# Stage one of a two-stage sequence kernel: one chunk of 128 tokens, or pairs of chunks with two tokens in a partition

## The chip, the cores and the metric

The kernel runs on one core of one Trainium2 chip. The time is that of the device in microseconds (us), from the runs of one program; a profile is one execution taken by the hardware profiler. The engines are PE (TensorE, matrix products), DVE (VectorE), ACT (ScalarE), POOL (GpSimd) and SP (SyncE, which issues most transfers). [...]

## The reference

Two layers stand one behind the other, on 4 batches, 768 tokens, 8 heads of 48 channels. The first is a recurrence with a decayed state; the second a gated long convolution, done with a Fourier transform over the tokens.

```python
for t in range(S):
    cur = np.einsum('bhd,bhe->bhde', u[None] * kt, vt)
    y[:, :, t] = np.einsum('bhd,bhde->bhe', rt, state + cur)
    state = wt[:, :, :, None] * state + np.einsum('bhd,bhe->bhde', kt, vt)
...
proj = x @ w_proj                       # (b, s, 3 * 384) -> x1, x2, x3
x2_conv = irfft(rfft(x2) * rfft(filter))
out = (x1 * x2_conv * x3) @ w_out
```

## The kernel before

**Stage one** takes the tokens in 24 chunks of 128, six a batch, with a token in each partition. For one chunk the program's steps have these names, which also stand in the order below:

- `lw`, `lk`, `lr`, `lv` load w, k, r and v (192 KB each). In the memory a token's 48 channels of one head lie together, so a load is made of packets of 192 bytes (`group`, L1425 to L1438). From the third group on, half of the v loads are issued by GpSimd and turned to bf16 on the way.
- `ln` takes the logarithm of w (ACT); `cs` sums it over the tokens of the chunk with two products by a triangular mask, 128 x 384 each, and four products of one column that give the whole chunk's decay (PE, L1473 to L1476); `ex` takes the exponential in PSUM (ACT); `kq` multiplies it by k and r (DVE, L1486); `ph` makes the decay of the state.
- `tr` turns keys and queries with eight transposes (PE, L1501), and `qk` copies them out of PSUM (ACT or DVE). For the last eight chunks a DMA on SP's queue may do both.
- `sc` makes the scores, eight products of 48 rows, two heads side by side in the two halves of the array's rows (PE, L1519). `mt` copies them with the mask (DVE) or without, and then `mc` cuts them on GpSimd.
- `kv` and `ki` make the next state (PE, L1560, L1566), `su` decays it (DVE).
- `rk`, `ru`, `rh`, `cc`, `vc` work out the token's own term with u (GpSimd and DVE).
- `yi`, `ys`, `y` add up the output in PSUM: the token's own term, the state's part and the scores times the values (PE, L1580, L1589, L1597). `xn` copies it out, `yt` turns it, `xT` stores it as the input of stage two, for some of the last chunks again by DMA.

**Stage two** works a batch at a time, once its six chunks are there: `p` and `q` project x1 and x3 (PE, L1768), `xw` projects x2 with tokens in partitions (L1809), `sd` folds the two halves of the sequence, `f` is the Fourier transform (L1655), `u` and `p<batch>` the product with the filter's spectrum, `E` the inverse transform (L1865), `aE`, `dE`, `yE` put its halves together and gate them, `o` is the last projection (L1950) and `so` the store. The Fourier tables `F` and `mi` are made in the kernel: angle maps on DVE and GpSimd (`ang`, `ia`), sines on ACT (`sin`, `is`), with ACT's function table loaded anew before and after.

**The order** of all steps is written out by hand in `ORDER`, a list of some 1,150 lines with the step, the engine that does it and, for what PE writes, the PSUM bank. Each engine runs its steps in that order. A line `warm n` gives PE products of zeros. SP's queue issues its transfers in order; one that waits holds those behind it, and an issue also waits for the one eight places ahead of it to land. Buffers turn: three sets of w, four of k and r, three of v.

Of the kernel before, what the change touches and what calls it, by code (L numbers as in the profile page):

```python
# [20 lines left out]
L = 128  # L21
# [4 lines left out]
DP = 64  # L26
# [10 lines left out]
ADD, DVE2, ACT2, POOL2, FOLD, WIDE = "V", "M", "N", "C", "Q", "X"  # L37

NLW, NLD, NG, NF, NS, NX, NO = 3, 4, 3, 4, 3, 3, 4
CASTS = (2,4,6,8,10,12,)  # L40
NV, NVL = 6, 3
NTURN = 8
# [6 lines left out]
warm 16 4  # L49
first A  # L50
imaps G
smalls D
zeros D
pads D
signs D
lw0 S
lw3 S
kz1 D
ln0 A
maske G  # L60
lw2 S
lr0 S
u S
maskn G smalls
maps G
ang2 D
ia0.0 G
ia1.0 G
maski G
kz0 G pads  # L70
ang1 D
ang0 D
ia2.0 D
cs0 P 2
lk0 S
ln2 A
ex0 A
ew0 -
kq0 D
warm 8 0  # L80
warm 6 1
cs3 P 0
ex3 -
ia2.1 D
kw0 -
lw1 S
ur A
warm 4 5
um P 6
warm 5 5  # L90
tr0 P 4
lk3 S
lr3 S
ew3 X
lr1 S
lk1 S
kz2 G
ph0 A
ub A
ln1 A  # L100
lv0 S
rk0 G ang0
kz3 G kq0
ru0 G
rh0 D
cc0 D
qk0 A
kq3 -
kw3 G rh0
lv2 G cc0  # L110
warm 3 5
cs1 P 5
warm 3 7
sc0 P 3
mt0.1 D
mc0.1 -
lr2 S
lk2 S
vb0 G
vc0 G rh0  # L120
ex1 A
ph3 A
mt0.0 D
ew1 -
lv3 G
warm 3 7
cs2 P 0
warm 4 7
tr3 P 4
ex2 A  # L130
kq1 D
qk3 A
kw1 -
warm 2 7
tr1 P 7
mc0.0 -
rk1 D
ru1 D
rh1 G rk1
qk1 D  # L140
ph1 A
warm 3 2
sc3 P 4
kv0 P 2
su0 D
ew2 -
kq2 D
kw2 -
lv1 S
warm 2 3  # L150
sc1 P 6
yi0 P 2
y0 P
mt1.1 D
lw4 S
mt3.1 -
xn0 A
xa0 -
mt3.0 N
ph2 A  # L160
rk2 D
ru2 D
rh2 G rk2
vb1 A
tr2 P 3
warm 3 2
ki1 P 5
warm 2 2
kv1 P
lw5 S  # L170
lk4 S
lr4 S
qk2 A
ln3 A
mt1.0 D
cc1 D
yt0 P 2
lr5 S
lk5 S
lv5 S  # L180
warm 3 4
sc2 P 0
su1 D
warm 1 3
ki2 P 5
kv2 P
cc2 D
su2 D
cs4 P 6
ex4 A  # L190
wproj1 G
mc3.1 -
ki3 P 4
kv3 P
mt2.1 A
mc1.1 -
ia0.1 G
vc1 D
xT0 D
warm 2 3  # L200
yi1 P 2
ys1 P
vc2 G
mt2.0 D
mc1.0 -
y1 P
ew4 -
su3 D
mc2.1 G mt1.0
kq4 D  # L210
mc2.0 -
cs5 P 0
xn1 A
ex5 A
warm 1 4
yi2 P 3
ys2 P
y2 P
kw4 -
kq5 D  # L220
ew5 -
lw7 S
ph4 A
xn2 A
tr4 P 6
xa1 -
xa2 -
kw5 -
qk4 D
yt1 P 3  # L230
tr5 P 2
yi3 P 6
qk5 D
yt2 P 4
ph5 A
wproj0 G kq4
mc3.0 C
lv4 S
xT2 D
ys3 P  # L240
lr7 S
y3 P
xn3 D
sc4 P 4
mt4.0 D
xa3 -
trig A
sin2 A
rk3 G qk4
ru3 G qk5  # L250
warm 1 0
yt3 P 7
xT1 D
mt4.1 A
ia1.1 G mt4.0
warm 3 0
sc5 P 5
mt5.1 -
lw6 S
mt5.0 M  # L260
xw0.0 P 0
rh3 D
cc3 D
vb3 G rh3
sin1 A
vc3 G mt5.0
ki4 P 2
cxw0.0 D
xT3 A
warm 1 3  # L270
xw0.2 P 6
sin0 A
kv4 P
is A
cxw0.2 D
su4 D
warm 5 4
p0.2.0 P 5
p0.0.0 P 0
table A  # L280
lr6 S
lk6 S
lk7 S
mc4.1 G
filt S
lw8 S
lw9 S
cp0.0.0 D
yi4 P 6
yi5 P 2  # L290
ys5 P
lv7 G cxw0.2
mc5.0 -
mc5.1 -
ys4 P
y5 P
lk9 S
lk8 S
mc4.0 -
y4 P  # L300
xn4 D
if1 A
ln4 A
xn5 A
lv8 S
cs6 P 0
xa5 -
yt5 P 3
if0 A
ex6 A  # L310
lr9 S
xa4 -
yt4 P 2
xT5 D
xT4 D
cs7 P 6
ew6 -
kq6 D
ex7 A
ew7 -  # L320
xw0.4 P 2
lr8 S
kq7 D
ph6 A
cxw0.4 A
sd0.1.0 D
kw7 -
sd0.0.0 D
rk4 G
p0.2.1 P 4  # L330
cp0.2.1 A
ph7 A
kw6 -
lw10 S
p0.0.1 P 0
tr7 P 3
qk7 D
fsd0 D
fsd1 D
tr6 P 7  # L340
ru4 D
cp0.0.1 A
qk6 A
cp0.2.0 A
lv9 S
f0.2 P 0
cf0.2 A
sc6 P 6
mt6.1 -
mc6.1 -  # L350
mt6.0 N
f0.0 P 4
sc7 P 2
cf0.0 A
warm 2 0
h1 P 0
ln5 A
lv6 G sd0.1.0
h2 P 6
rh4 G fsd1  # L360
mt7.1 -
mt7.0 M
mc7.0 -
hc1 A
mc7.1 -
cc4 D
h0 P 2
hc2 A
kv6 P 4
hg1 D  # L370
hg2 D
hc0 A
cs8 P 0
su6 D
mc6.0 C
vc4 G
warm 2 5
yi6 P 6
y6 P
ex8 A  # L380
ew8 -
hg0 D
xn6 A
yi7 P 4
ys7 P
y7 P
xn7 A
xa7 -
xa6 -
cs9 P 6  # L390
kq8 D
yt6 P 3
ki7 P 2
kv7 P
su7 D
wproj2 G
yt7 P 4
xT7 D
ex9 A
xT6 A  # L400
kq9 D
kw8 -
rk5 G
ph8 A
ru5 D
rh5 D
cc5 D
ew9 -
tr8 P 5
ki8 P 2  # L410
qk8 A
ph9 A
vb5 G xT7
vc5 G
xw1.0 P 0
cxw1.0 A
kw9 -
tr9 P 3
qk9 A
kv8 P  # L420
sc8 P 4
su8 D
mt8.1 -
lw11 S
f0.1 P 0
ki9 P 6
kv9 P
mt8.0 M
if2 A
lk10 S  # L430
lk13 S
mc8.0 -
cf0.1 A
sc9 P 2
su9 D
q0.2.1 P 7
lr10 S
mt9.0 N
lk11 S
lr11 S  # L440
mt9.1 -
mc9.1 -
q0.0.1 P 5
lr13 S
yi9 P 0
q0.2.0 P 4
yi8 P 2
xq0.0.1 -
u10.0 D
lw12 S  # L450
ys9 P
ln6 A
ys8 P
cq0.0.1 D
lw13 S
mc8.1 -
y8 P
lv11 G su9
mc9.0 C
warm 5 2 192  # L460
y9 P
cs10 P 5
lr12 S
lv12 S
xq0.2.1 -
u00.0 D
xq0.2.0 -
xn8 A
xn9 A
q0.0.0 P 2  # L470
cq0.2.0 D
cq0.2.1 D
xq0.0.0 -
xa8 -
lk12 S
lv10 G
rk6 G
cq0.0.0 D
xa9 -
gq0.0.0 -  # L480
yt9 P 4
ex10 A
xT9 A
ru6 D
kq10 D
yt8 P 7
xT8 A
cs11 P 0
ex11 A
if3 A  # L490
kq11 D
warm 1 4
xw1.2 P 2
ew10 -
kw10 -
lk15 S
lv13 S
rh6 G ru6
cc6 D
ph10 A  # L500
lr15 S
gq0.2.0 -
lw15 S
lr14 S
p1.2.0 P 4
tr10 P 7
p1.0.0 P 5
cxw1.2 A
qk10 A
ew11 -  # L510
kw11 -
ph11 A
cp1.2.0 A
cp1.0.0 A
tr11 P 2
q1.0.0 P 0
ki10 P 3
sc10 P 4
xq1.0.0 -
ln7 A  # L520
p0.0 D
lw14 S
mt10.1 A
gq0.0.1 -
qk11 D
sc11 P 6
kv10 P
lv15 G
mt11.0 A
vc6 G  # L530
mc10.1 G kq11
mc11.0 G qk11
q1.2.0 P 2
xq1.2.0 -
cq1.0.0 D
mt10.0 D
mt11.1 D
cs12 P 0
rk7 G qk11
ru7 G  # L540
yi10 P 4
ex12 A
ew12 -
su10 D
lv19 G qk11
ys10 P
mc10.0 -
y10 P
lv14 G
mc11.1 -  # L550
cs13 P 6
gq0.2.1 -
cq1.2.0 D
kq12 D
xn10 A
ex13 A
yi11 - 2
ys11 P
y11 P
lk14 S  # L560
xn11 V
E0.0 P 4
kq13 D
ew13 -
kw13 -
ph12 A
gq1.2.0 -
vb7 A
xa10 -
kw12 -  # L570
tr12 P 0
lw17 S
lw16 S
rk8 G
cE0.0 A
aE0.0.1 D
ru8 G
yt10 P 1
E0.1 P 2
xT10 D  # L580
aE0.0.0 D
aw0.0.0 -
qk12 A
ph13 A
xa11 -
cE0.1 A
kv12 P 1
su12 D
aE0.1.0 D
tr13 P 7  # L590
E0.2 P 4
qk13 A
cE0.2 A
aE0.1.1 D
aw0.1.1 -
yt11 P 0
ki13 P 1
kv13 P
lk16 S
aw0.1.0 -  # L600
rh7 D
sc13 P 2
ln8 A
aw0.0.1 -
xT11 D
su13 D
sc12 P 6
mt12.0 N
aE0.2.0 D
aE0.2.1 D  # L610
mt13.1 D
mc13.1 -
mc12.0 C rh7
lv16 S
lw19 S
p1.0.1 P 0
mt12.1 -
cs14 P 4
xw1.4 P 6
dE0.0.1 -  # L620
mt13.0 D
q1.0.1 P 2
cp1.0.1 A
p1.2.1 P 1
cc7 D
ex14 A
# [1422 lines left out]
```

## Time and profile before

| | us |
|---|---|
| median of 3 runs | 157.27 |
| lowest and highest | 157.26, 158.64 |
| the profiled execution's own time | 157.08 |
| its span, first to last instruction | 155.3 |

The profile gives each engine's busy time; a strip of 40 slices of the span (3.9 us each) with the busy share in tenths; the chain of waits, which is followed back from the last instruction to what released it; groups of instructions by line, engine and operation (busy time of all, mean of one in ns, idle time before them and what ended it); and windows, the same busy times for a stretch of the span. In rows of windows the columns are PE, weight loads, DVE, ACT, POOL, the granted clock of PE, DMA's share (over 1 where packets of two queues overlap) and GB/s. L-numbers are lines of the program; a helper's line stands for all who call it: L1328 is a product of two tensors, L1332 a copy on ACT.

### The profile page before, as it was taken

How to read it: one execution, taken by the hardware profiler on the slowest of the kernel's cores; microseconds unless marked ns; L12 is line 12 of the kernel's file. 1: busy time of each engine (PE TensorE's matmuls, PEld its weight loads, DVE VectorE, ACT ScalarE, POOL GpSimd, SP SyncE). 2: the span in 40 equal slices, each digit the busy share in tenths (PEclk: the TensorE clock that was granted, in tenths of full speed). 3: DMA queues.
4: the chain of work that ended last, by engine and by line, in shares of the span. 5: the costliest groups of instructions: out<-in, count | busy, mean ns of one | idle time of the engine just before them, and what ended most of it. 6: DMA issues, size and time to landing. Idle time of an engine off the chain costs nothing.

```text
span 155.3 us, 4220 instructions
## 1 busy us (share of the span) xinstructions
PE 142.3 (92%) x1634; PEld 89.4 (58%) x1634; DVE 135.5 (87%) x258; ACT 117.5 (76%) x195; POOL 102.0 (66%) x106
## 2 busy tenths in 40 slices
PE   7999894999999999999799999999999997999860
PEld 2455554656646767666566676665666664666430
DVE  4849984696999998999999999999999988799950
ACT  4584774897899894999879989989965575667650
POOL 6679595968229479589957988678796650802600
PEclk9999999699999999999999999999999999999997
DMA  5999999979999999899999918999997535000784
GB/s 105 227 212 218 194 145 215 200 135 339 177 187 213 198 181 180 142 199 176 187 192 201 179 25 144 220 193 189 178 183 149 155 122 209 0 0 34 294 330 159
DMA packets 112534, 27.12 MB, mean 175 GB/s; under 512 B 108545, under 2 KB 111106, under 8 KB 112514
## 3 DMA queue, kind: packets, MB, share of 16 engines
q1 hardware_dynamic: 98434, 24.49, 73.9%
q0 software_dynamic: 14080, 2.36, 20.0%
q8 instruction: 13, 0.21, 0.6%
q14 instruction: 7, 0.06, 0.1%
HBM read 22.41 MB, written 4.72 MB: 175 GB/s over the span
## 4 chain that ended last, share of the span: by engine, by line
PE 65%; DVE 11%; DMA 9%; ACT 4%; SPq 4%; issue 2%; DVEq 0%; ACTq 0%
PE banks L1768 13%; PE banks L1655 10%; PE banks L1380 7%; PE banks L1809 6%; PE banks L1950 5%; DMA kr<-in_k_dram 4%; PE banks L1865 4%; PE banks L1501 4%; SPq L1438 4%; PE banks L1519 4%; PE banks L1597 3%; DMA w<-in_w_dram 3%; DMA xT<-xn 3%; PE banks L1589 2%; PE banks L1473 2%
## 5 line engine op out<-in xcount | busy, mean ns | idle before, releaser
L1768 PE MATMUL banks<-xT,wproj 128*128 128x384 bf16 x144 | 27.3, 326 | 1.1 <-DVE xT L1334 1.0
L1328 DVE TENSOR_TENSOR kq<-banks,kr 128x768 bf16<-128x768 f32 x23 | 21.6, 950 | 3.1 <-DMA kr<-in_k_dram 2.7
L1328 POOL TENSOR_TENSOR vc<-vb,cc 128x768 bf16<-128x768 bf16 (+1 forms) x12 | 18.7, 1562 | 6.0 <-DVE sd L1820 3.1
L1328 POOL TENSOR_TENSOR rk<-kr 128x768 bf16<-128x768 f32 (+1 forms) x11 | 19.5, 1773 | 4.1 <-DMA kr<-in_k_dram 2.1
L1332 ACT ACTIVATE x<-banks 128x768 bf16<-128x768 f32 (+1 forms) x26 | 17.5, 687 | 5.2 <-PE banks L1809 3.0
L1482 ACT ACTIVATE banks<-banks 128x768 f32<-128x768 f32 x23 | 18.2, 798 | 1.9 <-PE banks L1476 1.6
L1535 DVE TENSOR_TENSOR mt<-banks,mask_excl 128x512 bf16<-128x512 f32 (+1 forms) x24 | 18.1, 772 | 1.3 <-PE banks L1519 1.1
L1768 PEld LDWEIGHTS <-wproj 128*128 128x128 bf16 x144 | 13.5, 98 | 9.3 <-issue 1.2
L1380 PE MATMUL banks<-wt 128*128 128x512 bf16 (+1 forms) x56 | 16.9, 397 | 1.1 <-DVE scl L1394 1.1
L1809 PE MATMUL banks<-wproj,xT 128*128 128x384 bf16 x72 | 13.7, 326 | 1.5 <-DMA xT<-xn 1.0
L1435 POOL DMA_DIRECT2D vb<-in_v_dram x12 | 11.3, 938 | 4.6 <-DVE sd L1820 3.3
L1540 POOL TENSOR_SCALAR_AFFINE_SELECT mt<-mt 128x512 bf16<-128x512 bf16 (+1 forms) x14 | 11.6, 834 | 3.5 <-ACT mt L1332 3.5
L1950 PE MATMUL banks<-wout,y 128*128 128x384 bf16 x72 | 13.3, 326 | 0.7 <-DVE y L1328 0.4
L1655 PE MATMUL banks<-sd,F 128*128 128x384 bf16 (+1 forms) x96 | 13.7, 328 | 0.0
L1501 PE MATMUL banks<-ident,kq 128*128 128x128 bf16 x144 | 11.1, 222 | 2.6 <-DVE kq L1328 2.1
L1332 ACT ACTIVATE qk<-banks 128x1024 bf16<-128x1024 bf16 x12 | 12.3, 1023 | 1.1 <-PE banks L1501 0.9
L1444 ACT ACTIVATE lg<-w 128x768 bf16<-128x768 f32 (+1 forms) x13 | 10.4, 798 | 3.2 <-DMA w<-in_w_dram 3.1
L1455 POOL TENSOR_TENSOR rk<-rk 128x384 bf16<-128x384 bf16 (+1 forms) x8 | 7.4, 921 | 7.7 <-DVE rk L1328 7.6
L1332 ACT ACTIVATE X<-banks 128x768 bf16<-128x768 f32 x12 | 9.8, 815 | 3.0 <-PE banks L1655 2.9
L1501 PEld LDWEIGHTS <-kq 128*128 128x128 bf16 x144 | 9.0, 98 | 4.9 <-DVE kq L1328 2.9
L1655 PEld LDWEIGHTS <-F 128*128 128x128 bf16 (+1 forms) x120 | 8.4, 103 | 5.6 <-issue 1.0
L1328 DVE TENSOR_TENSOR U<-X,hh 128x2304 bf16<-128x2304 bf16 (+1 forms) x12 | 11.6, 982 | 0.0
(118 smaller groups left out, 338.3 us busy)
## 6 DMA issues: line engine op xcount, KB each, us to landing
w<-in_w_dram SPq DMA_DIRECT2D x24, 192.0 KB, 4.2
kr<-in_r_dram SPq DMA_DIRECT2D x24, 192.0 KB, 4.5
kr<-in_k_dram SPq DMA_DIRECT2D x24, 192.0 KB, 4.5
out_dram<-o SPq DMA_DIRECT2D x9, 384.0 KB, 2.9
v<-in_v_dram SPq DMA_DIRECT2D x12, 192.0 KB, 4.0
vb<-in_v_dram POOLq DMA_DIRECT2D x12, 96.0 KB, 5.5
U<-in_moe_filter_fft_dram SPq DMA_DIRECT2D x1, 1152.0 KB, 6.0
wproj<-in_moe_w_proj_dram POOLq DMA_DIRECT2D x3, 288.0 KB, 5.1
```

Of the source, the lines that this page charges most:

```text
L1328: return eng(e).tensor_mul(o, a, b)
L1332: return nc.scalar.activation(out=o, in_=a, func=AF.Copy)
L1380: nc.tensor.matmul(banks[:, at, lo:hi], wt[:, 0:L], x, start=True, stop=True)
L1435: op(f"lv{i}", [POOL], lambda e, bk, q=q, rw=rw: nc.gpsimd.dma_start(out=vb[fv][:, q], in_=v[b, :, rw, :].rearrange("h t d -> t h d")), w= ...
L1482: return nc.scalar.activation(out=o, in_=x, func=AF.Exp)
L1501: nc.tensor.transpose(p[:, HP * m + j, :], kq[f][:, m, 2 * j:2 * j + 2, :], ident)
L1535: return copy(ACT, o, x) if e in (ACT, ACT2) else nc.vector.tensor_mul(o, x, _mid(mask_excl, z - HP * a))
L1540: return nc.gpsimd.affine_select(out=o, in_=o, pattern=[[0, z - HP * a], [1, L]], compare_op=ALU.is_gt, fill=0.0, base=0, channel_multipli ...
L1655: nc.tensor.matmul(p[rows], F[:, ti, c0 + rows.start:c0 + rows.stop], x[q][:, ti, :], start=(ti == 0), stop=(ti == NT - 1),)
L1768: nc.tensor.matmul(p, wproj[:, cb, col0:col0 + L], xT[bx][:, cb, sl], start=(cb == 0), stop=(cb == CB - 1),)
L1809: nc.tensor.matmul(view(bk)[:, z], xT[bx][:, cb, (c0 + z) * L:(c0 + z + 1) * L], wproj[:, cb, C:2 * C], start=(cb == 0), stop=(cb == CB - 1),)
L1950: nc.tensor.matmul(view(bk)[:, z], yt_[:, z, :], wout[:, cb, :], start=(cb == 0), stop=(cb == CB - 1),)
```

## The change

Stage one goes in pairs of chunks. A partition holds two neighbouring tokens: partition p of the pair has tokens 2p and 2p+1 (called j = 0, 1), so the first 64 partitions hold the first chunk and the other 64 the second (called x). Loads of k, r and v take both tokens of a head at once, 96 numbers or 384 bytes; w is loaded as before. GpSimd's casting loads of v go down from twelve to two.

All products of stage one then have 64 rows, 64 columns or both: the part of a chunk lies in 64 partitions, and the output of a chunk's half goes to 64 partitions. `cs` of the first j makes both chunks' decays; `kv` makes both chunks' states in two banks; a product `yx` is new, the part of the state that belongs to the other half of the rows. The mask `later` replaces the cut of GpSimd by a product. `xn` and `xT` work on a pair. Turning by DMA, `qk` and `xT` on SP, is open to all chunks: ten `qk`, each now two transposes of 64 partitions, and seven `xT` with twelve transposes in all, where there were six and five.

Within a chunk the tokens now stand even ones first. The Fourier tables' angles (`maps`, `imaps`), the load of the filter and the last projection follow that; the last projection writes 64 columns at a time, so that a store still has two neighbouring tokens in a partition.

`ORDER` is new as a whole (some 950 lines). The tables' steps stand ahead of the first logarithm, the first w loads behind the first k and r loads, and PE starts with 36 products of zeros of 512 columns (37 of 512 and 19 of 256 before, spread over the kernel).

```diff
-    kr = tiles(NLD, [L, 2, 2, H, D], FP32, "kr")
+    kr = tiles(NLD, [L, 2, H, 2, D], FP32, "kr")
...
+        def pair(x):
+            return x[b, :, rows, :].rearrange("h (p j) d -> p h j d", j=2)
...
+            op(f"l{name}{gi}", [SP], lambda e, bk, m=m, t=t: nc.sync.dma_start(out=kr[sl][:, m], in_=pair(t)),
+               w=[f"{name}.{sl}"])
...
+            def cs(e, bk):
+                p = two(bk, f"cs{i}")
+                for a, m in enumerate((mask_neg, mask_excl)):
+                    for x in (0, 1):
+                        nc.tensor.matmul(p[part[x], a, 0:C], m[:, j, :], lg[fg][:, x, :, 0:D], start=True, stop=True)
+                if j == 0:
+                    for x in (0, 1):
+                        for h in range(H):
+                            c = C + HP * x + h // 2
+                            nc.tensor.matmul(p[part[h % 2], 1, c:c + 1], lg[fg][:, x, h, :], ones, start=True, stop=True)
...
+                for a in range(HP):
+                    for par in (0, 1):
+                        p0 = DP * par
+                        for x in (0, 1):
+                            nc.tensor.matmul(
+                                p[part[x], par, a, :], turned(bk, p0, 0, x, a, j), both(bk, p0, x, a),
+                                start=True, stop=True,
+                            )
...
+        def kvc(e, bk):
+            for j in (0, 1):
+                for h in range(H):
+                    for x in (0,) if final else (0, 1):
+                        nc.tensor.matmul(
+                            kvp(bk, x)[part[h % 2], h // 2, :], kq[fk[j]][part[x], 0, h, :], vb[fv][part[x], h, j, :],
+                            start=(j == 0 and h < 2), stop=(ci + x == 0 and j == 1 and h >= H - 2),
+                        )
...
+        def across(e, bk):
+            for a in range(HP):
+                for j in (0, 1):
+                    for x in (0, 1):
+                        p0 = DP * (1 - x)
+                        nc.tensor.matmul(
+                            yat(bk, x)[part[j], 2 * a + 1 - x, :], turned(bk, p0, 1, x, a, j),
+                            state(x)[p0:p0 + D, a, :], start=(a == 0), stop=False,
+                        )
...
+        def yy(e, bk):
+            for j in (0, 1):
+                for h in range(H):
+                    for x in (0, 1):
+                        nc.tensor.matmul(
+                            yat(bk, x)[:, h, :], mt[fs[j]][part[x], HP * (h % 2) + h // 2, :], vb[fv][part[x], h, j, :],
+                            start=False, stop=(j == 1 and h == H - 1),
+                        )
...
-                            nc.tensor.matmul(
-                                view(bk)[:, z], yt_[:, z, :], wout[:, cb, :],
-                                start=(cb == 0), stop=(cb == CB - 1),
-                            )
+                            for x in range(n):
+                                o, lo = (view(bk)[:, z], 0) if n == 1 else (view(bk)[DP * x:DP * x + DP, z], L * x + DP * z)
+                                nc.tensor.matmul(
+                                    o, yt_[:, lo:lo + L // n], wout[:, cb, :], start=(cb == 0), stop=(cb == CB - 1))
...
+warm 20 7
+um P 0
+ub D
...
+sin0 A
+sin2 A
+is A
+table A
+ln0.1 A
+ln0.0 A
+warm 50 7
+cs0 P 0
```

More of the change, by code (lines that the diff above doesn't have):

```diff
@@ L156 @@
+qk0 A
+ph1 A
+lw6 S
+su0 D
+ki1 P
+tr2 P 4
+qk2 A
+kq3 D
+kv1 P 6
+su1 D
+ki2 P
+tr3 P 4
+tr1 P 2
+qk1 A
+sc1 P 0
+mt1.0 D
+mt1.1 D
+lk3 S
+yx0 P 2
+mc1.1 -
+sc0 P 0
+mt0.0 M
+mc1.0 -
+ln2 A
+cs5 P 0
+ex5 A
+mt0.1 -
+su2 D
+kq5 D
+wproj0 G
+yi0 P
+rk2 G
+ru2 G
+lw8 S
+cs4 P 0
+ex4 A
+mc0.1 -
+mc0.0 -
+ys0 P
+kq4 D
+y0 P
+ki3 P
+vb2 G
+qk3 A
+sc3 P 4
+ph2 A
+yx1 P 0
+yi1 P
+ys1 P
 mt3.1 -
 xn0 A
[L158 to L170, printed above, removed]
```

2331 lines of the change are left out of this document (1049 added, 1282 removed).

## The prediction

> **What bounds the kernel now.** I began with the page: its span, the busy shares, the strips of clock and DMA, the queues and the chain's shares.
>
> ```profile
> span 155.3 us, 4220 instructions
> PE 142.3 (92%) x1634; PEld 89.4 (58%) x1634; DVE 135.5 (87%) x258; ACT 117.5 (76%) x195; POOL 102.0 (66%) x106
> PEclk9999999699999999999999999999999999999997
> DMA  5999999979999999899999918999997535000784
> q1 hardware_dynamic: 98434, 24.49, 73.9%
> PE 65%; DVE 11%; DMA 9%; ACT 4%; SPq 4%; issue 2%; DVEq 0%; ACTq 0%
> ```
>
> The run that gave these rows took 157.08 us, so 1.8 us lie outside the span; the median of the three runs is 157.27, so it is a usual run. PE ends most waits, but 92% is an average. Three pieces of the chain of waits cut the span: the last scores-times-values product of batch 0 (L1597), and the wait in front of it.
>
> ```profile
> 1.11 3.60 PE banks L1380 x8
> 18.69 6.65 DMA kr<-in_k_dram
> 36.41 0.32 PE banks L1597 x8
> 126.44 3.90 DMA xT<-xn
> ```
>
> Cut there, and at 125.4, where the last such product ends, the windows say:
>
> ```profile
> core 0: us, PE busy (x) PEld busy (x) DVE busy (x) ACT busy (x) POOL busy (x), PEclk, DMA share, GB/s
> 0.00:37.00 37.00, 32.57 (x358) 18.89 (x359) 27.22 (x73) 24.97 (x39) 28.56 (x47) 0.95 1.08 193
> 37.00:125.40 88.40, 86.72 (x1121) 57.07 (x1120) 85.79 (x136) 75.73 (x131) 65.65 (x53) 1.00 1.09 180
> 125.40:155.30 29.90, 23.05 (x163) 13.48 (x159) 22.44 (x51) 16.76 (x27) 7.83 (x8) 0.96 0.36 136
> ```
>
> The **front** (to 36.7) is bound by loads: DMA is over-full (1.08), PE fills with warm-up matmuls, and one load alone is waited for 6.65 us. The **middle** is bound by PE and VectorE at once, 98% and 97%, with DMA still at 1.09. In the **tail** loads are over, and batch 3's stage two runs through PE and VectorE in turn.
>
> **PE, stage by stage.** Matmul rows overlap, so I price PE by pieces of the chain, where one begins as the other ends.
>
> ```profile
> 53.62 0.45 PE banks L1501 x8
> ...
> 54.64 1.10 PE banks L1655 x12
> 55.73 0.19 PE banks L1566
> 55.92 0.24 PE banks L1560 x8
> 56.16 0.33 PE banks L1519 x8
> ...
> 58.22 0.49 PE banks L1768 x3
> 58.71 0.17 PE banks L1580 x2
> 58.88 0.31 PE banks L1589 x16
> 59.18 0.30 PE banks L1597 x8
> ...
> 60.03 0.20 PE banks L1597 x8
> ```
>
> Eight products (L1597) cost 0.20, but 0.30 right behind L1589, which uses half the rows: changing the form of the array costs 0.10 us. Less that, 12 matmuls of 64 columns and 384 elements (L1655) take 1.00, 83 ns each, where a full one (L1768) takes 163: two halves run side by side. So do two of L1589 (0.20 for 16, 12.5 each), L1519 (0.23 for 8, 28 each), L1560 (0.14 for 8; I take 16 each, since a run's first pair starts late). No row shows four 64x64 quarters. Fully side by side, a group of four costs what a pair does now; if only two overlap, it costs two pairs. I take four: two already start together on either axis.
>
> Counting instructions of both kernels: the cumulative sums go from 48x163 to 96x83 (+0.1), their one-column sums from 96x25 to 192x16 (+0.7), PE's key turns from 144x56 to 112x56 (-1.8, the rest goes to DMA), scores from 192x28 to 384x14 (0), state products from 160x16 to 256x8 and 64x16 (+0.5), the new crossing products 192x8 (+1.5), the vc products from 32x85 to 96x42 (+1.3), L1589's from 160x12.5 to 96 (-0.8), L1597's from 192x25 to 384x12.5 (0), turns of x from 57x56 to 36x56 (-1.2), inverse transforms -0.3. Output matmuls become halves, two at a time: nothing. That is 0; but changes of form fall from 110 to 77, -3.3. Stage two is priced like L1768. Summed so, PE has 121.4 us of work before and 118.4 after (warm-up left out).
>
> [...]
>
> **The other engines.**
>
> ```profile
> L1328 DVE TENSOR_TENSOR kq<-banks,kr 128x768 bf16<-128x768 f32 x23 | 21.6, 950 | 3.1 <-DMA kr<-in_k_dram 2.7 <-ACT banks L1482 0.2
> L1482 ACT ACTIVATE banks<-banks 128x768 f32<-128x768 f32 x23 | 18.2, 798 | 1.9 <-PE banks L1476 1.6
> L1535 DVE TENSOR_TENSOR mt<-banks,mask_excl 128x512 bf16<-128x512 f32 x20 | 13.2, 682 | 0.4 <-PE banks L1519 0.4
> L1535 DVE TENSOR_TENSOR mt<-banks,mask_excl 128x1024 bf16<-128x1024 f32 x4 | 4.9, 1221 | 0.9 <-PE banks L1519 0.7
> L1332 ACT ACTIVATE qk<-banks 128x1024 bf16<-128x1024 bf16 x12 | 12.3, 1023 | 1.1 <-PE banks L1501 0.9
> L1458 DVE TENSOR_REDUCE cc<-rk 128x16 f32<-128x384 bf16 x11 | 6.0, 545 | 0.1
> L1609 DVE TENSOR_TENSOR xn<-banks,vc 128x384 bf16<-128x384 f32 x8 | 4.3, 553 | 0.8 <-PE banks L1597 0.7
> ```
>
> VectorE takes nearly all masks: 19 of 1221 and 5 of 682 for 4 and 20 (+8.1), and seven reductions over twice the elements (0.95 by this row, +2.7); it loses ten xn (-5.5), half its qk copies and ru products, seven xT, four of the inverse's sums: priced like that about -6 of 135.5. ScalarE loses eleven masks and ten xT, and gains pair-wide xn copies: about -6. GpSimd loses ten casting DMAs and ten cuts. None becomes the bound, and nothing is late in their place.
>
> **Loads.** In the first of these windows packets are of 192 bytes, in the second of 3072:
>
> ```profile
> 10.00:15.00 5.00, 4.73 (x62) 2.67 (x60) 4.32 (x8) 3.37 (x6) 4.52 (x5) 1.00 1.12 220
> 145.00:150.00 5.00, 4.58 (x28) 2.20 (x26) 4.05 (x13) 3.19 (x5) 1.38 (x2) 1.00 0.71 273
> ```
>
> 220/1.12 over 16 engines is 12.3 bytes per ns, 15.6 ns a packet; 273/0.71 gives 128 ns for 3072. On that line 384 bytes cost 23 ns (between 15.6, as per packet, and 31, as per byte). Per pair of chunks 8192 packets x 15.6 become 2048 x 15.6 + 3072 x 23: 8.0 us of DMA to 6.4 (5.0 to 8.0). In return DMA turns 20 half blocks of keys and 12 of x, for 6 and 5; SP's queue issues them, and an issue that waits there for its keys holds the loads behind it. I put that at nothing, since loads then run ahead; if that cover is gone, PE waits for about one landing, 3.90.
>
> **The front, after.** The order puts the Fourier tables first.
>
> ```profile
> L1444 ACT ACTIVATE lg<-w 128x768 bf16<-128x768 f32 x11 | 9.3, 847 | 1.8 <-DMA w<-in_w_dram 1.6
> L1672 ACT ACTIVATE F<-o,mpi 128x768 bf16<-128x768 uint16 x3 | 2.8, 931 | 0.0
> L1643 DVE TENSOR_SCALAR o<-o,tcol 128x384 int32<-128x384 f32 x3 | 1.4, 481 | 0.0
> L1661 ACT ACT_TABLE_LOAD x1 | 1.3, 1283 | 0.8 <-PEq L2033 0.8
> L1672 ACT ACTIVATE mi<-U,mpi 128x1152 bf16<-128x1152 uint16 x1 | 1.2, 1249 | 0.0
> ```
>
> Ten 512-wide warm-ups at 0.45 (3.60 for 8) end at 5.5, then the u product and its copy on VectorE to 6.3. Behind these VectorE has an index map, an angle map of two 481s, memsets of about 0.6 and another angle map: 9.2. ScalarE follows with two sines, the 1249, a table of 1283 and two half logs: cs0 at about 14.7. Both w halves of pair 0 stand behind four 384 KB loads: (4x23 + 2x15.6) x 64 packets per engine is 7.9 us, landed near 11, hidden by the sines. Then three pairs go through ScalarE and VectorE, each with some 17.5 us of queue up to that point: kq0 is out 2.6 after cs0, both qk of pair 0 at 8.2, its masks at 11.3, kq4 at 13.6, pair 1's masks at 16.8, pair 2's at 20.3. So the third pair's product ends near 35.4 instead of 36.7. By then PE has 14.4 of its 118.4 behind it, against 17.4 of 121.4 before.
>
> **The sum.** 104.0 us of PE work remain in both. Before, the rest of the span took 118.6; the middle is 97% full on VectorE, which now has about 4 us less in it, and a shortened DMA. I take 1.6 off (0 to 4): 117.0. 35.4 + 117.0 = 152.4 of span, and 1.8 outside: **154.2 us**. The front can be 32 (loads set it, sines earlier) to 40.
>
> **Rivals.** (1) *The middle gains in full*: with DMA and VectorE relieved, PE goes at 95% to the end, 104.0/0.95 + 5 behind the last matmul = 114.5; with a front of 33, 149 us. For: 1.09 DMA in the middle. Against: PE is 98% busy there already.
> (2) *PE goes cold in front, slower than before.* 25 warm-ups end near 11.5 and cs0 comes at 14.7; then PE has 14.4 us of work in 20.7. This window holds the long load wait of the kernel before:
>
> ```profile
> 20.00:30.00 10.00, 7.82 (x112) 5.42 (x112) 6.82 (x13) 6.25 (x11) 8.04 (x8) 0.84 1.12 186
> ```
>
> If the clock stays halved through the front, 14.4 becomes 28.8, and the third product comes some 6 to 8 us later: 161 us. It decides from about 40% of the front at half clock on. Against: the chain there waits for ScalarE and VectorE mostly. [...]
> (3) *Quarters run as two pairs*: 96 groups of scores x 56, 64 of states x 32, 48 crossings x 32 make 8.9 us more, nearly all in the middle where PE is full: 163. For: no row of four. Against: pairs start together on both axes.
> (4) *Nothing gained*: wide packets cost twice, loads as before, the earlier front is eaten by the waits in the new order: 157.
>
> **Chances.** Forecast 0.53 (its own range 151 to 158; 0.40 of it below 155.7), (1) 0.13, (2) 0.15, (3) 0.09, (4) 0.10. The mark of 1%, about what a measurement of this kernel can tell, lies at 155.7 and 158.8. Faster 0.40 + 0.13 = 0.53; same 0.12 + 0.08 = 0.20; slower 0.27 from (2), (3) and the edges. The range reaches from (1) to just short of (2): 149 to 160.5.
>
> **What will show it.** cs0 near 14.7 behind the table load; the third product of the sums (now 32 matmuls) near 35; crossing products at 8 to 10 ns each and scores at 14 to 15, not twice that; DMA's share in the middle below 0.9 in place of 1.09; VectorE near 129 busy; the last product some 34 us before the end, for 25.7 us of PE work follow it in the new order. I am wrong if the clock strip shows a half-rate stretch in front, if PE waits for a DMA turn in the middle, or if the rest takes longer than 119.

## The result: 241.8 us, half as long again, and the profile after

The changed kernel takes 241.8 us (median of 4 runs, 238.59 to 242.37) where the kernel before takes 157.75 beside it on the same chip (4 runs, 157.26 to 158.64). The ratio is 1.52, with a 95% interval of 1.50 to 1.54. Ratios here and below leave out runs that lie over 1.5% above the fastest of the same kernel; the profiled runs of the changed kernel and of j1 are among these, as are three of j1's six. The forecast was 154.2 us, its range 149 to 160.5.

The profiled run is the one of 242.37 us. These are the lines of its page that answer to those of before:

```profile
span 240.7 us, 5855 instructions
PE 171.6 (71%) x2507; PEld 107.8 (45%) x2507; DVE 133.7 (56%) x226; ACT 112.8 (47%) x169; POOL 93.7 (39%) x94
PEclk9985655699569957579779985899889869979999
DMA  6999990699930000590599336894432515100083
```

No engine is full any more, and none has much more to do than before: VectorE's busy time is 133.7 against 135.5, ScalarE's 112.8 against 117.5, GpSimd's 93.7 against 102.0. PE is busy longer, 171.6 against 142.3, but the strip shows its clock at half rate in many slices, where before it was full in all but two. The DMA strip, before full up to two thirds of the span, has holes, one of four slices (72 to 96 us).

The windows of after, cut at the same two events as before (the third pair's product of scores and values, and the last such product), tell where the time went:

```profile
0.00:47.90 47.90, 34.33 (x558) 22.42 (x558) 27.65 (x65) 23.80 (x31) 27.79 (x46) 0.71 0.83 190
47.90:195.20 147.30, 106.35 (x1742) 68.11 (x1736) 80.70 (x111) 71.93 (x111) 57.15 (x40) 0.82 0.55 111
195.20:240.70 45.50, 30.93 (x233) 17.24 (x225) 25.32 (x51) 17.09 (x29) 8.81 (x9) 0.94 0.28 96
```

The front is 10.9 us longer than before (47.9 for 37.0), the middle 58.9 (147.3 for 88.4), the tail 15.6 (45.5 for 29.9), together the 85.4 us by which the span grew. In each stretch I take PE's busy time from its length. The rest, in which PE stood still, was 4.4, 1.7 and 6.9 us before, and is 13.6, 41.0 and 14.6 now: 56.1 us more. The other 29.3 us are busy time, and PE's clock was 0.71, 0.82 and 0.94 in the three stretches, before 0.95, 1.00 and 0.96. So two thirds of the loss is PE with nothing to do; the other third is longer busy time, which goes with the lower clock.

The groups of instructions of after show that what they do costs what it did, and that they wait (the last figures of a row are the idle time before them and what ended it):

```profile
L1379 DVE TENSOR_TENSOR mt<-banks,later 128x1024 bf16<-128x1024 f32 (+1 forms) x24 | 26.2, 1109 | 19.6 <-PE banks L1365 17.8
L1126 DVE TENSOR_TENSOR kq<-banks,kr 128x768 bf16<-128x768 f32 x24 | 22.5, 955 | 24.8 <-ACT banks L1312 24.7
L1312 ACT ACTIVATE banks<-banks 128x768 f32<-128x768 f32 x24 | 18.8, 796 | 36.1 <-PE banks L1306 18.8
```

The product of keys with the exponentials took 950 ns before and takes 955; the exponential 798 and 796. But the idle time in front of the first went from 3.1 us to 24.8, in front of the second from 1.9 to 36.1. PE waits for VectorE or ScalarE, VectorE for the exponential (L1312), the exponential for PE's sums (L1306), the masks (L1379) for PE's scores: a ring in which each engine waits in its turn for another.

One such wait in detail. This is the timeline of ScalarE in after (start, duration; in brackets the idle time before it and its releaser):

```profile
82.24 2.35 ACT L1312 ACTIVATE banks<-banks 128x768 f32<-128x768 f32 x3 [5.94 <-PE banks L1306]
86.52 0.80 ACT L1312 ACTIVATE banks<-banks 128x768 f32<-128x768 f32 x1 [1.93 <-PE banks L1301]
87.23 0.81 ACT L1130 ACTIVATE xn<-banks 128x768 bf16<-128x768 f32 x1
```

and this that of PE:

```profile
80.00 0.56 PE L1460 MATMUL banks<-vb,mt 64*128 64x48 bf16 x32
85.63 0.53 PE L1301 MATMUL banks<-lg,mask_neg 128*64 128x384 bf16 x2 [2.58 <-DVE kq L1126]
88.09 2.13 PE L1518 MATMUL banks<-sd,F 128*64 128x384 bf16 x12 [1.60 <-ACT xn L1130]
```

`ORDER` has here, with what lies between left out:

```
y3 P
...
cs12 P 6
ex12 A
cs11 P 4
...
cs10 P 0
ex10 A
ex11 A
kq11 D
kq10 D
cs13 P 4
ex13 A
...
xn3 A
kq13 D
f0.1 P 2
```

`xn3` copies out what `y3` has left in its bank at 80.6 us. ScalarE is idle then, and stays so until 82.24. But in its queue `xn3` stands behind four exponentials. The last of them, `ex13`, needs the sums `cs13`, and PE can't make these before VectorE's `kq11` has freed bank 4. So `xn3` runs at 87.23, 6.6 us after it could have, and PE's next work, `f0.1`, waits for the bank that `xn3` frees: PE does nothing for 2.58 us in front of `cs13` at 85.63, and again for 1.60 in front of 88.09.

### The profile page after: what moved, and what is told of

It reads as the page before. It is cut to its first block, busy times and chain, and to the rows that moved or that the text cites. A ratio compares the mean times of both kernels' runs of the same rounds, so it can differ in the third digit from the quotient of the medians.

```text
span 240.7 us, 5855 instructions
## 1 busy us (share of the span) xinstructions
PE 171.6 (71%) x2507; PEld 107.8 (45%) x2507; DVE 133.7 (56%) x226; ACT 112.8 (47%) x169; POOL 93.7 (39%) x94
## 4 chain that ended last, share of the span: by engine, by line
PE 28%; DVE 13%; ACT 8%; issue 3%; DVEq 0%; ACTq 0%
PE banks L1518 6%; PE banks L1635 5%; PE banks L1819 5%; PE banks L1676 3%; PE banks L1732 3%; DVE mt L1379 3%; ACT x L1130 2%; PE banks L1301 1%; DVE g L1661 1%; ACT banks L1312 1%; ACT hh L1596 1%; DVE U L1126 1%; PE banks L1365 1%; DVE kq L1126 1%; DVE y L1126 1%
## 5 line engine op out<-in xcount | busy, mean ns | idle before, releaser
L1379 DVE TENSOR_TENSOR mt<-banks,later 128x1024 bf16<-128x1024 f32 (+1 forms) x24 | 26.2, 1109 | 19.6 <-PE banks L1365 17.8
L1126 DVE TENSOR_TENSOR kq<-banks,kr 128x768 bf16<-128x768 f32 x24 | 22.5, 955 | 24.8 <-ACT banks L1312 24.7
L1312 ACT ACTIVATE banks<-banks 128x768 f32<-128x768 f32 x24 | 18.8, 796 | 36.1 <-PE banks L1306 18.8
L1126 POOL TENSOR_TENSOR vc<-vb,cc 128x768 bf16<-128x768 bf16 x12 | 17.7, 1472 | 29.1 <-DVE rk L1273 12.1
L1126 POOL TENSOR_TENSOR rk<-kr 128x768 bf16<-128x768 f32 x10 | 18.1, 1812 | 23.9 <-DVE P L1591 9.1
L1661 DVE TENSOR_TENSOR g<-banks,x 128x768 bf16<-128x768 f32 (+1 forms) x14 | 11.0, 786 | 21.1 <-PE banks L1635 12.2
L1635 PEld LDWEIGHTS <-wproj 128*128 128x128 bf16 x144 | 14.6, 104 | 17.8 <-issue 11.2
L1301 PE MATMUL banks<-lg,mask_neg 128*64 128x384 bf16 x48 | 10.1, 403 | 13.3 <-ACT lg L1261 8.1
L1365 PE MATMUL banks<-qk 48*64 48x128 bf16 x384 | 11.9, 264 | 8.6 <-DVE mt L1379 2.7
L1819 PE MATMUL banks<-wout,y 128*64 128x384 bf16 (+1 forms) x138 | 14.3, 340 | 4.8 <-DVE y L1126 1.9
L1365 PEld LDWEIGHTS <-qk 48*64 48x64 bf16 x384 | 8.7, 132 | 12.6 <-issue 7.2
L1130 ACT ACTIVATE qk<-banks 128x1024 bf16<-128x1024 bf16 x11 | 11.2, 1025 | 5.6 <-PE banks L1328 5.6
L1130 ACT ACTIVATE xn<-banks 128x768 bf16<-128x768 f32 (+1 forms) x13 | 9.8, 761 | 8.2 <-PE banks L1460 8.2
L1126 POOL TENSOR_TENSOR rk<-rk,u_b 128x768 bf16<-128x768 bf16 x8 | 13.1, 1632 | 0.3
```

The costliest lines, as they stand in the source:

```text
L1126: return eng(e).tensor_mul(o, a, b)
L1130: return nc.scalar.activation(out=o, in_=a, func=AF.Copy)
L1301: nc.tensor.matmul(p[part[x], a, 0:C], m[:, j, :], lg[fg][:, x, :, 0:D], start=True, stop=True)
L1312: return nc.scalar.activation(out=x, in_=x, func=AF.Exp)
L1365: nc.tensor.matmul(p[part[x], par, a, :], turned(bk, p0, 0, x, a, j), both(bk, p0, x, a), start=True, stop=True,)
L1379: return copy(ACT, o, x_) if e in (ACT, ACT2) else nc.vector.tensor_mul(o, x_, _mid(lat, HP * (z - a)))
```

## The experiments

Two theories stand at the start. **Order**: the new layout's work fits into about the old time, but in `ORDER`, as it is now written, steps that could run stand in the in-order queues behind steps that wait. **Clock**: PE falls to half rate in the front, and as nothing fills its waits any more (before, 27 places of `ORDER` had products of zeros, now three), it never recovers. A third is the **layout** itself: its narrow tiles, wide packets and longer chain from sums to masks cost more than I put down.

### The same steps in another order

In e1 every step keeps its engine, its tiles and its DMAs. Only the order of the queues and the PSUM banks are dealt anew: of the steps whose inputs are there, each engine takes the first of a priority list, worked out with durations from the traces. Products of zeros stand at the start alone. The same was done with the layout of before, as a control.

```diff
 y3 P
-sd0.0.0 G
-su9 D
-ln5 A
...
-cs13 P 4
-ex13 A
-kq12 D
...
+cq0.2.0 D
+rk5 G
+q0.2.1 P 7
+su8 D
 xn3 A
+mt9.0 M
+ki9 P
```

> The changed kernel with every operation, engine, tile, packet and DMA kept, and only the order of the operations and their PSUM banks dealt anew: each engine takes next, among the operations whose inputs and banks are ready, the first of a priority list, with the durations of the profile of the changed kernel; no fillers in PE's gaps. Theory 'order' (the written order makes the in-order queues wait for each other, and PE's clock falls in those waits): 150 to 162 us; worked from the profile's durations it comes to 153. Theory 'layout' (pairs, 64x64 tiles and their hand-offs are themselves dearer): over 200 us, since each of them is still there. Theory 'clock alone': the same as 'order' here, with a granted clock over 0.93.

> The kernel before, with its operations, engines, tiles and loads kept and its order dealt anew in the same way as in the first run, its fillers left out but those at the start. It sets what this way of ordering is worth: 150 to 164 us under every theory (worked from the profile's durations 154). Theory 'layout is neutral': within 3% of the first run. If it lies far above the first run, the changed layout is the better one; far below, the worse.

e1 took 182.5 us (4 runs, 181.12 to 191.99), 1.168 of the kernel before (1.154 to 1.182). So 59 of the 84 us go with the order (and the banks, which are dealt with it). The time lies between what was expected of "order" and of "layout", and meets neither. Its page, and its windows, cut where the third product and the last one begin:

```profile
PE 146.0 (81%) x2506; PEld 91.9 (51%) x2506; DVE 143.6 (79%) x226; ACT 113.6 (63%) x169; POOL 99.8 (55%) x94
PEclk9996599999999999999997599969999999999998
DMA  5999999999999999769999365925366534004225
```

```profile
0.00:39.10 39.10, 31.30 (x572) 20.58 (x572) 28.23 (x69) 29.20 (x40) 30.91 (x48) 0.91 1.04 228
39.10:146.40 107.30, 89.66 (x1719) 57.56 (x1718) 88.28 (x111) 68.59 (x103) 60.39 (x39) 0.95 0.83 163
146.40:180.80 34.40, 24.99 (x220) 13.81 (x218) 27.07 (x48) 15.83 (x26) 8.54 (x8) 0.98 0.28 98
```

The clock is back to 0.95 in the middle though no product of zeros stands there, the DMA strip has no hole before 100 us, and PE's busy time fell by 25.6 us with the same work.

The control, the layout of before in an order dealt the same way, took 180.6 us (179.14 to 181.86), 1.156 (1.136 to 1.176). This says two things. The way of dealing is worse than the order that the kernel before came with, by 22 us on the same layout. A part of this can be the products of zeros, which the kernel before has at 27 places and the control at one; but the control's clock is low up to 39 us only (0.69), and 0.97 in the 138 us behind, so they aren't the most of it. And dealt alike, both layouts take about the same. So e1's 182.5 is no measure of what the new layout can do, and what separates it from 157 isn't shown to be the layout.

### The clock alone

e2 keeps after's order in every queue, and puts products of zeros into PE's waits, at 40 places.

```diff
 kq0 D
+warm 11 7
 cs2 P 4
...
 su0 D
+warm 4 1
 ki1 P
+warm 10 1
 tr2 P 4
...
 ln2 A
+warm 11 5
 cs5 P 0
```

> The changed kernel in its own order, with 40 groups of filler matmuls (359 of 256 columns, 38 us at full clock) put into PE's waits wherever a PSUM bank is free. Theory 'clock alone': 160 to 175 us, since the waits are filled and PE stays at full clock. Theory 'order': 215 to 235 us; the profile's durations on this order at full clock throughout come to 225, and 24 of the waits find no free bank and stay empty. Theory 'layout': no more than a few us below 240.

It took 233.2 us (one run). The page of e2:

```profile
PE 193.6 (84%) x2696; PEld 112.9 (49%) x2696; DVE 133.5 (58%) x226; ACT 113.2 (49%) x169; POOL 93.8 (41%) x94
PEclk9997997958999985999979999999889999999999
```

The clock is 0.941 over the span instead of 0.823, and the time falls by 9 us of 84 (by 5 against the fastest run of after). The same stall stands in the timeline of ScalarE in e2, nearly as long as before:

```profile
80.07 2.35 ACT L1352 ACTIVATE banks<-banks 128x768 f32<-128x768 f32 x3 [6.03 <-PE banks L1346]
84.02 0.80 ACT L1352 ACTIVATE banks<-banks 128x768 f32<-128x768 f32 x1 [1.60 <-PE banks L1341]
84.73 0.81 ACT L1170 ACTIVATE xn<-banks 128x768 bf16<-128x768 f32 x1
```

`xn3` runs 6.3 us after the end of `y3` at 78.4, where it was 6.7. A faster PE comes to the same waits earlier. The clock as the first cause falls. The 9 us are what could be had in this way and not the whole price of the clock, as the products of zeros take time of PE themselves (193.6 us busy for 171.6) and some waits found no free bank for them. In the front, where the clock had been lowest (0.60 from 15 to 37 us in after, 0.92 in e2), the third product starts at 46.2 instead of 47.5.

### Whose queue

e3 keeps PE's sequence of after as it is, and deals the other queues and the banks anew.

```diff
 y3 P
-sd0.0.0 G
-su9 D
...
 cs12 P 6
-ex12 A
+su9 D
+xn3 A
+lw16 S
+fsd1 D
+vb6 G
 cs11 P 4
...
 cs10 P 0
-ex10 A
-ex11 A
+ex12 A
```

> PE's own sequence is that of the changed kernel, operation by operation; the queues of ACT, DVE, POOL and SP and the banks are dealt anew as in the first run. Theory 'order', with the loss spread over the queues: 172 to 190 us (worked from the profile's durations: 176). If PE's sequence alone is the cause: about 240 us. If it lies in the other queues alone: about 155 us.

It took 195.74 us (one run): 46 of the 59 us that e1 gained are in the queues of ScalarE, VectorE, GpSimd and SP and in the banks, and 13 in PE's own sequence, if the two add up, which wasn't tried the other way round. The time is 6 us over the range that was expected.

### A few steps moved

The two sharpest trials of the order theory change nothing but the places of some steps within their queue. h25 moves 25 of the 778 steps, among them the pair of the stall above; h115 makes 115 such moves.

```diff
 vb0 G
+cs3 P 6
 tr0 P 0
...
 kv0 P 2
-cs3 P 6
 lw7 S
...
 cs10 P 0
-ex10 A
 ex11 A
+ex10 A
 kq11 D
...
 cs13 P 4
-ex13 A
 kq12 D
...
 xn3 A
+ex13 A
 kq13 D
```

> The changed kernel's own order with 25 of its 778 issued operations put a few places earlier or later in their engine's queue, one at a time, each where the profile's durations say that it waits or lets others wait (as ex13, which waits for PE on ACT while xn3 behind it could go); banks, engines and all else are kept. Theory 'order': 195 to 220 us (worked from the profile's durations: from 259 to 209 with PE's clock, from 224 to 193 at full clock). Theory 'layout' or 'loads': above 230, since no operation, load or tile is changed.

> The same with 115 such moves of about 107 operations, as far as single moves gain anything. Theory 'order': 172 to 192 us (worked: 178 with PE's clock, 170.5 at full clock), near what the first run's new order gave. Theory 'layout' or 'loads': above 230.

h25 took 206.93 us and h115 183.4 (one run each): 25 moves take 35 us off, 115 take 58, with banks and products of zeros as in after. Both lie in the range expected of "order". The place of the stall in h25, in the timelines of ScalarE and of PE:

```profile
80.25 0.83 ACT L1130 ACTIVATE xn<-banks 128x768 bf16<-128x768 f32 x1
81.26 0.80 ACT L1312 ACTIVATE banks<-banks 128x768 f32<-128x768 f32 x1 [0.18 <-PE banks L1301]
```

```profile
80.71 0.35 PE L1301 MATMUL banks<-lg,mask_neg 128*64 128x384 bf16 x2 [1.73 <-DVE kq L1126]
81.14 1.41 PE L1518 MATMUL banks<-sd,F 128*64 128x384 bf16 x12
```

`xn3` runs ahead of `ex13`, in what had been a wait, and `f0.1` follows `cs13` without one; that it now takes 1.41 instead of 2.13 is the clock. The strips of h115 answer another question:

```profile
PEclk9999696579996999999999999999999999999999
DMA  5999998919999900059799996599964633600474
```

The hole in the DMA strip is still there, three slices of 4.5 us from 64 us on. It comes from SP's queue, where a turn of keys waits for VectorE. In the waits of after it is this row:

```profile
SPq L1335 <- DVE kq L1126: 32.9, 3, 20.8
```

32.9 us in three waits, the longest 20.8, and the loads behind them start that much later. h115 keeps SP's queue as it is, and there this row is one wait of 11.2 us. From 62 to 79 us of h115 DMA's share is 0.16, and PE is still busy for 14.2 of the 17 us, at full clock: a hole of this length costs little. What the longer one of after costs by itself wasn't tried.

### A better order for both layouts

Both layouts then had their order searched for longer (h1, h2), and once more with the waits of VectorE and GpSimd for each other taken in the order of time (j1, j3). In h1 and j1 two casting loads of v (`vb10`, `vb11`) also move from GpSimd's DMA to a load on SP and a cast on ScalarE; every other step keeps its engine. The layouts, tiles and DMAs are else those of after and of before.

```diff
 y3 P
-sd0.0.0 G
-su9 D
...
 xn3 A
+yx4 P 2
+vc4 G
+yi4 P
+mt8.0 M
+ys4 P
+kq12 D
...
-lv10 -
...
-vb10 V
+lv10 S
+vb10 A
```

> The changed kernel with order and banks searched much longer, by small moves in the queues and of banks from a start like the first run's, against the durations, the DMA engines' time, PE's clock and the wait of VectorE for GpSimd; casts of v as in the run with the casts moved; all else kept. Theory 'order': 152 to 168 us (worked: 150 to 151), near the kernel before. Theory 'layout': stays near 180, where two new orders stood.

> The kernel before, its order searched in the same way and as long, fillers left out but those at the start. It sets what this search is worth on the layout before: 152 to 168 us (worked: 155). If both layouts are worth the same, within 3% of the run above; if the changed layout is dearer in ways the durations do not hold, the run above is slower by more than that.

> The changed kernel with order and banks searched once more, now with the waits of VectorE and GpSimd for each other taken in the order of time (the profile of the run before this one shows VectorE's bf16 operations up to 1.6 us longer in that search's order); engines as in the run with the casts moved, all else kept. Theory 'order': 152 to 160 us (worked: 153), at or below the kernel before. Theory 'layout': 165 or more, as the layout then costs what no order takes away.

> The kernel before with its order searched in the same way, its fillers left out but those at the start. Worked: 161; expected 156 to 170. If the changed layout gains by itself, this stands above the first run of this call; if it costs, below.

| order | layout of after, us | ratio to the kernel before | layout of before, us | ratio |
|---|---|---|---|---|
| dealt once (e1, control) | 182.5 | 1.168 (1.154 to 1.182) | 180.6 | 1.156 (1.136 to 1.176) |
| searched (h1, h2) | 171.19 | 1.083 (1.073 to 1.093) | 187.02 | 1.182 (1.172 to 1.192) |
| searched once more (j1, j3) | 167.94 | 1.043 (1.034 to 1.051) | 183.46 | 1.136 (1.124 to 1.149) |

(Medians of all 4 runs, of all 6 for j1.) The windows of j1, cut at the third product, which stands there in two parts and is done at 41.5, and where the last one begins:

```profile
0.00:40.50 40.50, 34.39 (x604) 20.67 (x606) 30.01 (x70) 30.24 (x41) 30.28 (x49) 0.92 1.03 231
40.50:140.00 99.50, 91.19 (x1725) 57.50 (x1717) 85.11 (x110) 70.31 (x107) 55.58 (x35) 0.93 0.82 166
140.00:169.80 29.80, 24.21 (x216) 13.97 (x207) 22.94 (x48) 14.50 (x25) 10.17 (x9) 0.95 0.40 142
```

The tail is back at before's 29.9, the middle stands at 92% PE, and the third product is done 4.6 us later than before (36.9). In each of the last two lines of the table the new layout is 8% cheaper than the old one; of that, the two moved casts may be 2% (f5 below has nothing else, and took 179.23 for e1's 182.5, in one run). So the layout isn't what costs the 84 us: j1, with the new layout and the two casts moved, lies some 7 us above the kernel before. It is no proof that it is the better one, as the search never found on the old layout what the kernel before has, and no kernel here beats that one.

These searches are a weak measure. On the old layout the longer ones (ratios 1.182 and 1.136) gain little or nothing on the single dealing (1.156). For all the new orders (e1, h1, j1, f1 below and the three of the old layout) the durations promised 150 to 161 us, and the runs took 168 to 187: a time worked out from durations is too low here as well. By the mark set ahead for j1, its 167.9 would even speak for a cost of the layout (165 or more); that j3 was promised 161 on the old layout and took 183.5 is why I don't read it so.

### Packets, GpSimd and more products of zeros

f1 deals the order of e1 once more, counting that VectorE and GpSimd hinder each other (last section) and a change of the array's form at 0.11 us; it has the two casts of v moved. f2 is f1 with each load of k, r and v as two, one for the even and one for the odd tokens, so with packets of 192 bytes again. f5 is e1 with nothing but the two casts moved. f3 is f1 with four groups of products of zeros.

```diff
-            op(f"l{name}{gi}", [SP], lambda e, bk, m=m, t=t: nc.sync.dma_start(out=kr[sl][:, m], in_=pair(t)),
+            op(f"l{name}{gi}", [SP], lambda e, bk, m=m, t=t: [nc.sync.dma_start(
+                out=kr[sl][:, m, :, j], in_=pair(t)[:, :, j]) for j in (0, 1)],
...
-vb10 V
+lv10 S
...
+vb10 A
...
+warm 50 7
```

(The first lines are f2's, those in the middle f1's and f5's, the last one of f3's.)

> As the first run, with the order and banks dealt anew once more, now counting what the first run's profile shows and the first priority list did not know: VectorE's operations on bf16 in SBUF (dE 0.35 to 1.06 us, yE 0.55 to 1.17) start only when a GpSimd operation that is running has ended, and a change of tile shape on PE costs 0.11 us. The casts of v of the last two pairs, which were DMAs by GpSimd, are a load by SP and a cast on ACT; all else is kept. Theory 'order': 158 to 172 us (worked from the durations: 159.5), that is most of what the first run still lacks of the kernel before. Theory 'layout': no better than the first run's 182.

> The run above with each load of k, r and v as two DMAs, one of the even and one of the odd tokens, so in packets of 192 bytes as before the change, in the same tiles and the same order. If the wide packets carry what the layout gains: 6 to 15 us slower than the run above, since 36 loads take some 0.6 us more of the DMA engines each, 21 us in all. If loads are covered outside the front: 0 to 5 us slower. If the DMAs bound neither: within 1 us.

> The first run's kernel, its order kept, with only the casts of v of the last two pairs moved from DMAs of GpSimd to a load by SP and a cast on ACT. If GpSimd's DMA was what held VectorE's rh9 (5.28 us for an operation of 0.35) and the waits behind it: rh9 under 2 us and the whole 3 to 8 us below the first run's 182. If not: rh9 again over 4 us and the whole within 2 us.

> The run two above with 4 groups of fillers (57 of 256 columns) in PE's longest waits. Theory 'order': 0 to 3 us faster, as little of PE's time is left at half clock. If the clock still holds it: 5 us or more faster.

f1 took 180.64 us (ratio 1.140, 1.130 to 1.150), f5 179.23 and f3 181.65 (one run each). So what VectorE and GpSimd cost each other is not what e1 lacks, nor are the two casts. f3 doesn't settle the clock: its own, 0.926, is no higher than f1's 0.951. f2 took 202.7 (1.279, 1.269 to 1.288), 22 us more than f1. The first windows of f1 and of f2, each about as long as its loads last:

```profile
0.00:95.00 95.00, 74.97 (x1307) 47.33 (x1308) 66.20 (x116) 65.58 (x96) 56.91 (x65) 0.93 1.00 217
```

```profile
0.00:118.00 118.00, 87.58 (x1441) 53.77 (x1441) 70.48 (x120) 67.16 (x97) 59.73 (x67) 0.87 0.96 181
```

The DMA engines are full in both, and the 23 us between these windows are about the 22 of the result; what lies behind takes 82.5 and 83.6 us. In f1's order loads set the pace up to 95 us, and there the wide packets are worth 22 us. (f2 also has 36 issues more in SP's queue. With the DMA engines at 0.96 I put the time down to the packets; the two weren't tried apart.)

## Why the prediction was wrong, point by point

**The step that failed is the sum.** It says "104.0 us of PE work remain in both. Before, the rest of the span took 118.6", and then "I take 1.6 off (0 to 4): 117.0". The rest took 192.8 (240.7 less 47.9). The 118.6 was no property of the work: it was what the work takes in an order in which PE stands still for 1.7 us in 88, and for 8.5 in the whole rest; in after's rest it stands still for 55.5. The change replaces that order as a whole. I priced the steps and carried the old order's density over to the new one, and of the rivals only the fourth spoke of waits in the new order, at the price of the gain and no more. That it was the order is shown for 58 of the 84 us and more: the same steps in another order take 182.5, the same order with 25 steps moved 206.9, with 115 moves 183.4. The mark I set, wrong "if the rest takes longer than 119", was the right one.

**Clock.** Rival 2 has its condition: PE stood still for 4.37 us in front of the first sums and the clock fell at 16.1 us, the front ran at 0.60 from 15 to 37 us and 0.51 to 47, and the strip has half-rate stretches up to the end. It hasn't its price: with the clock at 0.92 the third product came 1.3 us earlier, where I had put 6 to 8, and the whole kernel 9 us. A cold clock followed the waits; in e1 it is back without any filler behind the start. So the clock made the time worse, by some 9 to 29 us (an estimate, from e2's gain and from the growth of PE's busy time), and isn't where the loss began.

**Front.** I said 35.4 for the third product; it starts at 47.5. The first logarithms start at 14.88 and their sums at 15.87, near the 14.7 for `cs0`: the sines first cost what I counted. What came behind was mis-sized: I added up busy times of ScalarE and VectorE, 17.5 us of queue, as if neither waited for the other. In e1's order the third product starts at 39.1, and in j1's it is done at 41.5, so some 6 to 8 of the 12 us are order. The other 4 to 6 are the estimate's, and what they are isn't settled; DMA's share there is 1.03 to 1.04, so loads may set it. (The share passes 1 with SP's queue alone too: 1.15 from 6.8 to 10.2 us of after, where no other has a packet.)

**PE's prices were nearly right.** Behind the third product PE is busy for 114.7 us in e1, at a clock of 0.96, and for 109.8 before (some products of zeros included) at nearly full clock: about the same work in both, as the sum has it. (The counts of the prediction add up to 3.2 us less where the sum took 3.0; it changes nothing.) The timeline of PE in after, at full clock:

```profile
129.07 0.44 PE L1409 MATMUL banks<-vb,kq 64*64 64x48 bf16 x32
129.34 0.70 PE L1365 MATMUL banks<-qk 48*64 48x128 bf16 x32
129.98 0.26 PE L1420 MATMUL banks<-S,wide 128*128 128x192 bf16 x1
```

32 state products take 0.27 from start to start, 8.4 ns each (I had 8), with four quarters of the array side by side; as two pairs, at the 16 ns I had put for one of a pair, they would take 0.51 (an estimate), so rival 3 is out. 32 scores take 0.64, or 17 ns each if one change of form of 0.10 is taken off; I had 14 to 15.

**The other engines** came out near what was counted: VectorE's busy time at 133.7 for 129, ScalarE 112.8 for about 111.5, and none became the bound. It is just not busy time that bounds this kernel.

**Loads.** DMA's share in the middle is 0.55, under the 0.9 I named, but for the wrong reason: loads wait for buffers and behind SP's turns of keys. That "an issue that waits there for its keys holds the loads behind it" was put at nothing. It happens, 32.9 us of it; in h115, with 11.2 us of it, it does no great harm. Where an order is bound by loads, the wide packets are worth 22 us (f1 against f2), 1.8 for each of the twelve pairs, where I had counted 1.6 of DMA time. The price was about right; after's order never lets the loads be the bound.

**What stays open** is the last 4%: j1 at 1.043. Either the search is still short of what the kernel before has, or the layout costs something that only a tight order shows. The controls speak for the first, as the same search is 14% short on the old layout (in part perhaps for want of the products of zeros); nothing here shows it.

## What to carry to other kernels

When a change rewrites the order of in-order queues, the time of the old kernel is no base for the new one: the density of an order is part of its price, and a sum of durations is only a lower bound. Follow at least one stage of the new order queue by queue, and look for steps that are ready but stand behind one that waits for another engine: here the places of 25 of 778 steps cost 35 us. And test a new layout and a new order apart, the order with the old layout too, or the one gets the blame for the other.

## What the runs showed of the hardware that was not expected

**PE's clock went in steps of 3.41 us, at full or half rate.** In after the clock's stretches between the first change, at 16.10 us, and the last within the span, at 214.07, are whole multiples of this. Some windows of after, cut at these steps:

```profile
22.94:26.35 3.41, 1.88 (x52) 1.33 (x50) 1.22 (x2) 2.27 (x4) 3.33 (x3) 1.00 1.19 230
26.35:29.76 3.41, 1.78 (x48) 1.28 (x48) 1.29 (x2) 1.38 (x2) 0.49 (x1) 0.50 0.93 214
36.59:40.00 3.41, 3.08 (x78) 2.73 (x80) 2.65 (x4) 1.15 (x3) 0.00 (x0) 0.50 0.02 5
43.42:46.83 3.41, 3.41 (x101) 2.77 (x95) 2.39 (x3) 0.45 (x1) 3.31 (x4) 0.50 0.58 70
46.83:50.24 3.41, 2.20 (x68) 1.85 (x65) 1.81 (x2) 2.76 (x4) 3.33 (x3) 1.00 1.27 211
```

A step with PE busy 1.88 of 3.41 was followed by half rate; at half rate one with 3.08 didn't bring it back, and one with 3.41 did. PE's busy time in a step doesn't settle it, though: the step from 200.43 us, with 1.81, was followed by full rate, and the one from 173.13, at half rate with 2.84, too. What decides isn't known.

**VectorE and GpSimd held each other up.** The sums of two bf16 tensors on VectorE take 352 ns each in after, the first row, and 548 in the mean in e1, the second. There most still take about 350, and two that have GpSimd at work beside them take 2.05 us together:

```profile
L1785 DVE TENSOR_TENSOR y<-y 128x384 bf16<-128x384 bf16 x8 | 2.7, 352 | 0.0
```

```profile
L1784 DVE TENSOR_TENSOR y<-y 128x384 bf16<-128x384 bf16 x8 | 4.2, 548 | 0.0
```

In the timelines of e1, VectorE's and GpSimd's:

```profile
155.54 1.06 DVE L1686 TENSOR_TENSOR sd<-x 128x384 bf16<-128x384 bf16 x1
```

```profile
155.36 1.02 POOL L1686 TENSOR_TENSOR sd<-x 128x384 bf16<-128x384 bf16 x1
```

The step of VectorE, 0.35 us in the mean of the four of its form in before, takes 1.06 here and ends at 156.60, just behind GpSimd's at 156.38. In the timelines of f5, VectorE's first, a keys' product (L1125), which reads one operand from PSUM, isn't prolonged beside GpSimd's (0.94 us, and 0.947 in the mean of all 24), and the step behind it (L1272), with both in SBUF, is (1.31 us, where this step takes 0.35 in after):

```profile
92.51 0.94 DVE L1125 TENSOR_TENSOR kq<-banks,kr 128x768 bf16<-128x768 f32 x1
93.37 1.31 DVE L1272 TENSOR_TENSOR rk<-rk 128x384 bf16<-128x384 bf16 x1
```

```profile
92.64 1.82 POOL L1125 TENSOR_TENSOR rk<-kr 128x768 bf16<-128x768 f32 x1
```

GpSimd's steps are prolonged too. In f5 its step just before the one shown, here the second row, took 2.64 us, and VectorE's beside it, the first row, 2.85; the mean of their forms in after is 1.63 and 1.35:

```profile
88.34 2.85 DVE L1712 TENSOR_TENSOR P<-U 128x2304 bf16<-128x2304 bf16 x1
```

```profile
90.06 2.64 POOL L1125 TENSOR_TENSOR rk<-rk,u_b 128x768 bf16<-128x768 bf16 x1
```

Once in e1 a step of VectorE's took far longer, the first row VectorE's, the others GpSimd's:

```profile
94.22 5.28 DVE L1272 TENSOR_TENSOR rk<-rk 128x384 bf16<-128x384 bf16 x1 [1.23 <-POOL rk L1125]
```

```profile
94.14 3.55 POOL L1125 TENSOR_TENSOR rk<-kr 128x768 bf16<-128x768 f32 x2
97.66 1.62 POOL L1125 TENSOR_TENSOR rk<-rk,u_b 128x768 bf16<-128x768 bf16 x1
```

It waited through three steps of GpSimd one behind another, and PE behind it for 5.63 us. In f5, with the casts moved, GpSimd stands still for 1.08 us behind its step at 92.64, and the same step of VectorE takes 1.31. Why VectorE didn't come in between the three in e1 isn't known. All this is worth little here: f1, whose order counts it, has 8.6 us less of VectorE busy than e1 (135.0 for 143.6) and is 2 us faster.
